# Queueing two more zero regions ahead of the first gradient store, in a decode backward kernel whose output is mostly zeros

## The chip, the cores and the metric

The kernel runs on one core of a Trainium2 chip. The metric is the device time of one execution in microseconds. A single core shows no second die to compare with, so "slow" here only means a run more than 1.5% above the fastest run of the same kernel in the same rounds. Profiles are of one execution each; the span in a profile is some 1.8 us shorter than the time of the same run.

## The reference, cut to what matters

The reference computes one decode step (attention over a cached window, then a gated feed-forward block) and all its gradients. Only the last 4096 of 32768 cache rows are attended to, so seven eighths of the two cache gradients are zeros, and they must be written.

```python
Hq, Hkv, Sk, Dh = 32, 8, 32768, 128            # B = 2
W = min(4096, max(256, Sk // 4))               # 4096
k = jnp.repeat(k_cache[:, :, Sk - W:, :], rep, axis=1)
v = jnp.repeat(v_cache[:, :, Sk - W:, :], rep, axis=1)
scores = jnp.einsum("bhqd,bhkd->bhqk", q, k) * (Dh ** -0.5)
...
_out, _vjp = jax.vjp(_f, A_x, A_k_cache, A_v_cache, A_wq, ...)   # out_2, out_3: cache gradients
```

Each cache gradient has 16 slabs (2 batches, 8 heads). A slab is 28672 rows of zeros, 7 MiB, and 4096 rows of numbers, 1 MiB. That makes 32 zero regions of 7 MiB, and 32 MiB of computed gradient.

## The kernel before

GpSimd issues the zeros as DMAs that read a small zero tile. The first 27 regions are issued early in the kernel. The other five are cut into 15 pieces that go out one behind each store of a computed gradient. Three regions (8, 16, 24) are cut into parts of different numbers of rows. The intent is to give some of the 16 DMA engines more 8 KiB packets than others; the traces have the size of each packet (8192 bytes) but not its engine, so which engine gets how many is not shown.

```python
OFF_DUP = OFF_WD                                   # scratch at 164 KiB
OFF_ST = [OFF_WG, OFF_WG + 16 * KIB] + [i * 16 * KIB for i in range(4)] + [OFF_WQ, OFF_WQ + 16 * KIB]
...                                                # second store buffer: 152 to 168 KiB
ZERO_PARTS = {8: (...), 16: (...), 24: ((4, 1), (15, 2), (2, 2), (15, 18), (12, 1), (P, 4), (16, 4))}
ZERO_FIRST, ZERO_CUTS = 27, (3, 2, 2)

def zero_cast(i):
    dst, done = zero_regions[i].bitcast(F32), 0
    for rows, n in ZERO_PARTS.get(i, ((P, ZPK // P),)):
        src = zt[0:rows * (P // rows):P // rows, :]
        nc.gpsimd.dma_start(out=dst[...].rearrange("(p k e) -> p k e", p=rows, k=n),
                            in_=src.unsqueeze(1).to_broadcast([rows, n, ZE]))
...
for i in range(ZERO_FIRST): zero_cast(i)           # at the start of attention(0)
...
for n, (b, what) in enumerate(jobs):               # 4 jobs: dV, dK of batch 0, then of batch 1
    ...
    for gq in range(2):
        ...                                        # 16 x 2 matmuls and evictions into two store buffers
        for a in range(2):
            nc.gpsimd.dma_start(out=dst_v[:, b, g0:g0 + 2, :, :], in_=sts[a][:])   # a store of 2 MiB
            zero_next()                                                            # a zero piece
        if gq == 0 and n + 1 < len(jobs):
            nxt = bd_of(n + 1)                     # block matrix of the next job, through OFF_DUP
```

## Time and profile before

| what | number |
|---|---|
| median of 6 runs | 802.67 us (791.57 to 809.69) |
| span of the profiled run | 797.8 us |
| DMA traffic, mean rate | 332.43 MB, 417 GB/s |
| first gradient store issued | 628.52 us |
| DMA engines idle or half idle around it | 604 to 632 us |

The page's part on DMA issues tells how far the zero stream runs ahead (operation, count, size of each, median time from issue to landing):

```profile
out_dram<-zt POOLq DMA_DIRECT2D x24, 7168.0 KB, 105.0
out_dram<-mem POOLq DMA_DIRECT2D x16, 2048.0 KB, 26.6
```

A 7 MiB region lands 105 us after its issue though the engines need only 17 us for it: it waits in the queue behind about five others. So the time at which a DMA is issued says little here about when its bytes move, and a queue that is empty (1 GB/s from 622 to 629.5 us) is worse than one that is long.

### The profile page before, as it was taken

The numbers are of one execution on the slowest core, as the hardware profiler recorded it, in microseconds if no ns is written. First come the engines' busy times: TensorE is split into PE (matmuls) and PEld (weight loads), VectorE is DVE, ScalarE is ACT, GpSimd is POOL, SyncE is SP. The second block draws the span as 40 slices with busy tenths as digits, with TensorE's granted clock in tenths as the row PEclk, the third lists the DMA queues.
The fourth block names the chain that finished last, engine by engine and source line by source line (L and its number), as shares of the span: only waits on it lengthen the run. The fifth ranks groups of instructions, "written<-read, shape, count | busy, mean of one in ns | idle before, by whom it ended". The sixth has DMA issues, their size and how long they took to land. (4 is left out here: it accounts for less than half of the span.)

```text
span 797.8 us, 12459 instructions
## 1 busy us (share of the span) xinstructions
PE 567.8 (71%) x5096; PEld 302.4 (38%) x5096; DVE 473.7 (59%) x1161; ACT 281.2 (35%) x406; POOL 65.7 (8%) x96
## 2 busy tenths in 40 slices
PE   3899997787688999832856879888796837811800
PEld 3656553455566555312425444433241212200200
DVE  1699998137433899740912577855447959922810
ACT  1534330135345343101102436553443826810800
POOL 4300000000020000000030000000000111210110
PEclk9999999777797999885976959865595968975955
DMA  8999999999999999999999999999999599999998
GB/s 365 419 418 421 420 425 427 422 430 427 427 420 420 424 424 423 426 425 431 427 427 429 428 426 428 425 426 426 430 428 403 222 429 427 428 429 430 427 430 347
DMA packets 41177, 332.43 MB, mean 417 GB/s; under 512 B 2192, under 2 KB 2208, under 8 KB 2336
## 3 DMA queue, kind: packets, MB, share of 16 engines
q0 software_dynamic: 34176, 268.44, 87.8%
q1 hardware_dynamic: 6932, 63.19, 34.9%
q8 instruction: 40, 0.66, 0.3%
q10 hardware_dynamic: 12, 0.01, 0.1%
q14 instruction: 17, 0.14, 0.0%
HBM read 49.30 MB, written 282.33 MB: 416 GB/s over the span
## 5 line engine op out<-in xcount | busy, mean ns | idle before, releaser
L422 DVE TENSOR_TENSOR mem<-mem,ee 128x512 bf16<-128x512 bf16 x512 | 180.7, 414 | 37.3 <-PE M_ps L433 36.9
L433 PE MATMUL M_ps<-mem 128*128 128x512 bf16 x512 | 139.6, 390 | 6.4 <-DVE mem L422 6.1
L93 ACT CAST mem<-ps_g 128x512 bf16<-128x512 f32 x128 | 74.3, 586 | 72.4 <-PE ps_g L836 65.7
L836 PE MATMUL ps_g<-mem 128*128 128x512 bf16 x256 | 82.5, 417 | 20.0 <-DVE mem L91 11.6
L380 ACT COPY mem<-KT_ps 128x1024 bf16<-128x1024 bf16 x64 | 63.4, 1013 | 80.9 <-PE KT_ps L378 75.1
L91 DVE CAST mem<-ps_g 128x512 bf16<-128x512 f32 x128 | 82.9, 687 | 6.8 <-ACT mem L93 4.0
L114 POOL DMA_DIRECT2D out_dram<-zt x45 | 35.5, 1029 | 503.7 <-DMA out_dram<-zt 503.4
L378 PE MATMUL KT_ps<-ident_bf,mem 128*128 128x128 bf16 x512 | 47.3, 238 | 30.9 <-DMA mem<-in_A_k_cache_dram 26.0
L254 PE MATMUL ps_tb<-ident_bf,mem 128*128 128x128 bf16 x480 | 56.2, 251 | 9.5 <-DMA mem<-in_B_w_gate_dram 2.8
L433 PEld LDWEIGHTS <-mem 128*128 128x128 bf16 x512 | 43.6, 99 | 49.0 <-issue 15.0
L836 PEld LDWEIGHTS <-mem 128*128 128x128 bf16 x256 | 25.9, 103 | 76.3 <-issue 56.7
L93 ACT COPY mem<-ps_tb 128x512 bf16<-128x512 bf16 x44 | 25.8, 586 | 70.8 <-PE ps_tb L254 66.0
L254 PEld LDWEIGHTS <-mem 128*128 128x128 bf16 x480 | 37.4, 128 | 34.9 <-issue 30.7
L378 PEld LDWEIGHTS <-mem 128*128 128x128 bf16 x512 | 35.5, 107 | 36.8 <-DMA mem<-in_A_k_cache_dram 26.6
L656 PE MATMUL VT_ps<-ident_bf,mem 128*128 128x128 bf16 x512 | 45.9, 237 | 2.4 <-ACT mem L93 1.1
L665 PE MATMUL dP_ps<-mem 128*128 128x512 bf16 x128 | 43.6, 429 | 4.7 <-ACT mem L93 4.7
L656 PEld LDWEIGHTS <-mem 128*128 128x128 bf16 x512 | 36.1, 106 | 27.0 <-issue 19.0
L93 ACT COPY mem<-VT_ps 128x1024 bf16<-128x1024 bf16 x31 | 31.7, 1022 | 34.8 <-PE VT_ps L656 33.6
L91 DVE COPY mem<-ps_tb 128x512 bf16<-128x512 bf16 x44 | 18.6, 424 | 41.9 <-PE ps_tb L254 40.5
L727 PE MATMUL ps_gr<-mem 2*128 2x512 bf16 (+1 forms) x78 | 33.4, 492 | 12.7 <-DVE mem L747 10.0
L91 DVE CAST mem<-ps_gr 128x512 bf16<-128x512 f32 (+1 forms) x38 | 24.8, 656 | 27.6 <-PE ps_gr L727 27.6
L91 DVE COPY mem<-VT_ps 128x1024 bf16<-128x1024 bf16 x33 | 23.1, 700 | 27.4 <-PE VT_ps L656 26.9
(244 smaller groups left out, 632.0 us busy)
## 6 DMA issues: line engine op xcount, KB each, us to landing
out_dram<-zt POOLq DMA_DIRECT2D x24, 7168.0 KB, 105.0
out_dram<-mem POOLq DMA_DIRECT2D x16, 2048.0 KB, 26.6
out_dram<-zt POOLq DMA_DIRECT2D x10, 2048.0 KB, 30.7
mem<-in_A_k_cache_dram SPq DMA_DIRECT2D x16, 1024.0 KB, 21.9
mem<-in_A_v_cache_dram SPq DMA_DIRECT2D x16, 1024.0 KB, 23.0
out_dram<-zt POOLq DMA_DIRECT2D x5, 3072.0 KB, 26.4
out_dram<-zt POOLq DMA_DIRECT2D x3, 4096.0 KB, 62.5
out_dram<-mem SPq DMA_DIRECT2D x5, 1792.0 KB, 18.8
```

The source lines that it names most:

```text
L91: nc.vector.tensor_copy(out=out, in_=in_)
L93: nc.scalar.copy(out=out, in_=in_)
L114: nc.gpsimd.dma_start(out=dst[done * ZE:(done + rows * n) * ZE].rearrange("(p k e) -> p k e", p=rows, k=n), in_=src.unsqueeze(1).to_broadc ...
L254: nc.tensor.transpose(out=ps[:, a, :], in_=src_block(a), identity=ident_bf[:])
L378: nc.tensor.transpose(out=KT_ps[:, jj, :], in_=Kt[b, g][:, u * 8 + jj, :], identity=ident_bf[:])
L380: nc.scalar.copy(out=KT[:], in_=KT_ps[:])
L422: nc.vector.tensor_tensor(out=pk[:, :, i, :].rearrange("p j (d t) -> p j d t", t=2), in0=Kb[:, j0:j0 + pk_j, :].rearrange("p j (d t) -> p ...
L433: nc.tensor.matmul(out=M_ps[:], lhsT=Vt[b, g][:, j, :], rhs=pk[:, jj, :, :].rearrange("p i d -> p (i d)"), start=(j == 0), stop=(j == NJ - 1))
L656: nc.tensor.transpose(out=VT_ps[:, jj, :], in_=Vt[b, g][:, a * 8 + jj, :], identity=ident_bf[:])
L665: nc.tensor.matmul(out=dP_ps[:, c, :], lhsT=dOpad[:, w0:w0 + P], rhs=VT[:, c * 4:(c + 1) * 4, :].rearrange("d a k -> d (a k)"), start=(i = ...
L727: nc.tensor.matmul(out=ps[:, :n], lhsT=lhsT_fn(k), rhs=rhs_fn(k), start=True, stop=True)
L836: nc.tensor.matmul(out=ps[:, a2, :], lhsT=lhs_bf[:, jp * P:(jp + 1) * P], rhs=rhs_bd[:, ap * 2 + a2, gq * 4:(gq + 1) * 4, :].rearrange("q ...
```

## The change

Its intent is to have bytes in the queue at the time when the compute has not yet produced the first gradient tile.

```diff
-    ... 24: ((4, 1), (15, 2), (2, 2), (15, 18), (12, 1), (P, 4), (16, 4))}
-    ZERO_FIRST, ZERO_CUTS = 27, (3, 2, 2)
+    ... 24: ((3, 16), (15, 2), (3, 4), (15, 18), (12, 2), (P, 4))}
+    ZERO_FIRST, ZERO_CUTS = 29, (1, 1, 1, 2, 2)
```

(The entries of regions 8 and 16 on the first line of each pair are unchanged and cut here.)

More of the change, by code (lines that the diff above doesn't have):

```diff
@@ L105 @@
     ZPK = Z * DH // 2 // ZE
-    ZERO_PARTS = {8: ((4, 1), (15, 2), (2, 2), (15, 14), (12, 2), (P, 4), (16, 7)), 16: ((4, 1), (15, 2), (2, 2), (15, 14), (12, 2), (P, 4), (16, 7)), 24: ((4, 1), (15, 2), (2, 2), (15, 18), (12, 1), (P, 4), (16, 4))}
-    ZERO_FIRST, ZERO_CUTS = 27, (3, 2, 2)
+    ZERO_PARTS = {8: ((4, 1), (15, 2), (2, 2), (15, 14), (12, 2), (P, 4), (16, 7)), 16: ((4, 1), (15, 2), (2, 2), (15, 14), (12, 2), (P, 4), (16, 7)), 24: ((3, 16), (15, 2), (3, 4), (15, 18), (12, 2), (P, 4))}
+    ZERO_FIRST, ZERO_CUTS = 29, (1, 1, 1, 2, 2)
     def zero_cast(i):
```

## The prediction

> **What bounds the kernel now.** I read the page's slices first, because the kernel writes two gradients that are mostly zeros: 332.43 MB of DMA traffic in a span of 797.8 us.
>
> ```profile
> DMA  8999999999999999999999999999999599999998
> GB/s 365 419 418 421 420 425 427 422 430 427 427 420 420 424 424 423 426 425 431 427 427 429 428 426 428 425 426 426 430 428 403 222 429 427 428 429 430 427 430 347
> q0 software_dynamic: 34176, 268.44, 87.8%
> ```
>
> The reader is to see a flat rate of about 427 GB/s in 36 of 40 slices. Only the first (loads begin), the last (the stream ends) and slices 31 and 32, at 598 to 638 us, fall below. At 427 GB/s the 332.43 MB need 778 us, so the DMA engines are the bound and the other engines' waits are mostly free. Only time in which the DMA engines stand still can be won. I therefore cut the stretch around the dip into windows (the last two columns are the DMA share and GB/s):
>
> ```profile
> 604.00:612.00 8.00, 5.97 (x14) 1.71 (x13) 5.65 (x8) 3.22 (x4) 0.00 (x0) 0.50 1.07 412
> 612.00:622.00 10.00, 7.48 (x18) 2.26 (x18) 8.59 (x11) 4.59 (x8) 0.00 (x0) 0.55 0.77 320
> 622.00:629.50 7.50, 6.59 (x23) 2.10 (x22) 7.18 (x12) 6.47 (x12) 0.98 (x2) 1.00 0.00 1
> 629.50:632.00 2.50, 2.28 (x9) 0.76 (x8) 2.29 (x5) 2.26 (x5) 1.90 (x3) 1.00 0.92 367
> 632.00:740.00 108.00, 51.80 (x160) 16.05 (x159) 65.73 (x97) 45.61 (x79) 14.16 (x20) 0.75 1.09 428
> 740.00:792.00 52.00, 16.19 (x56) 5.14 (x54) 18.48 (x30) 16.24 (x29) 4.99 (x7) 0.70 1.08 428
> 792.00:794.00 2.00, 0.00 (x0) 0.00 (x0) 0.00 (x0) 0.00 (x0) 0.00 (x0) 0.50 0.90 381
> ```
>
> The zeros run out between 612 and 622 us, unevenly over the engines; nothing moves for 7.5 us; then the rate is full again to 792. The gap, counted against 428: (16 x 8 + 108 x 10 + 427 x 7.5 + 61 x 2.5) / 428 = 4562 / 428 = 10.7 us. Who ends it stands in GpSimd's timeline (start, duration, operation, idle before and what ended it):
>
> ```profile
> 19.33 7.64 POOL L114 DMA_DIRECT2D out_dram<-zt  x8 [0.31 <-POOL zt L315]
> 556.44 1.84 POOL L114 DMA_DIRECT2D out_dram<-zt  x2 [21.94 <-DMA out_dram<-zt]
> 628.52 0.73 POOL L844 DMA_DIRECT2D out_dram<-mem  x1 [70.24 <-ACT mem L93]
> 664.06 0.71 POOL L844 DMA_DIRECT2D out_dram<-mem  x1 [22.11 <-ACT mem L93]
> 695.64 0.72 POOL L130 DMA_DIRECT2D out_dram<-zt  x1 [2.08 <-DMA out_dram<-zt]
> 748.82 0.71 POOL L844 DMA_DIRECT2D out_dram<-mem  x1 [30.39 <-ACT mem L93]
> ```
>
> The last two early zero regions are issued at 556.4 us. The first cache gradient store is issued at 628.5, when ScalarE has evicted its last tile. In between GpSimd has nothing to give. The first line also shows that eight issues go out at once and the later ones wait for landings: I take it that an issue waits for the eighth before it. Piece 9 at 695.64 fits: the eighth before it is piece 5, which ends 12 + 14 = 26 MiB after the first store begins, 629.7 + 26 x 2.45 = 693.4 us.
>
> Last, VectorE's timeline shows where the stores hold the compute back:
>
> ```profile
> 648.04 0.20 DVE L274 COPY mem<-qsT 128x128 bf16<-128x128 bf16 x1 [8.54 <-DMA out_dram<-mem]
> 732.21 0.20 DVE L274 COPY mem<-qsT 128x128 bf16<-128x128 bf16 x1 [29.52 <-DMA out_dram<-mem]
> ```
>
> The four jobs (dV, dK of each batch) need block matrices, built from a scratch at 164 KiB. That scratch lies inside the second of the eight store buffers (152 to 168 KiB), so it waits for store 1 to land (648.0), and for store 9 (732.2). Stores are numbered 0 to 15, four to a job.
>
> [...] In 606 to 610 us, where wq gradient stores of SyncE run beside the last zeros, the trace agrees that they share:
>
> ```profile
> q0 software_dynamic: 134, 1.09, 72.6%
> q1 hardware_dynamic: 81, 0.60, 35.7%
> ```
>
> [...]
>
> **The change part by part.** (1) Two regions of 7 MiB move ahead of the first store. A MiB takes 1.049 MB / 428 GB/s = 2.45 us, so they are 34.3 us of work. They cover the gap of 10.7 us and push all stores back by the rest. The bytes are the same. (2) Three regions remain; in pieces of 1, 1, 1, 2, 2 MiB they give 15 pieces, still one behind each of the first 15 stores, 21 MiB in place of 35. (3) Region 24 is cut anew. [...] A packet takes 8192 B / 26.75 GB/s = 0.31 us. [...] It is 46 early issues for 45.
>
> The intent of (3) follows from the windows: the gap today forgives imbalance. The engines that finish first, between 612 and 622, wait, and all start level at 629.7. Without the gap, an engine that is early stays early to the end, so it must be given more.
>
> Now the new order in time. Without a gap the work up to the first store would have ended at 629.7 - 10.5 = 619.2 us (10.5 is the gap without the last window's start). Two regions more: the stores' data start at S = 653.5. Then (2.46 us per MiB, which matches 67 MiB from 629.7 to 794.5 before, and 1.2 us from data to landing as at store 1):
> - store 1 has landed after 5 MiB: 653.5 + 12.3 + 1.2 = 667.0, not 648.0. VectorE's wait of 8.5 us becomes about 27; both jobs behind it move by 19 us.
> - store 4 followed that landing by 16.0 us (664.06 - 648.04), so it is issued at 683.0. The queue holds stores 0 to 3 and pieces 0 to 3, 13 MiB, until 685.5. Issue to first data is 1.2 us: margin 1.3 us.
> - store 9 has landed after 20 + 12 = 32 MiB: 733.4 or so, against 732.2. Its wait falls from 29.5 to about 12 us.
> - store 12 followed by 16.6 us: issued at 750.0. The queue holds 24 + 16 = 40 MiB, until 751.9. Margin 0.7 us after the first data.
> - the end: 53 MiB after S, 783.9, against 794.5 before.
>
> Eight in flight harms nothing: the last zeros can be issued from about 560 us, and store 3 needs region 27 landed (about 637), yet comes at 640. The sum on the path: -10.6 us; packets of region 24, 0 to -0.9; bubbles at stores 4 and 12, 0 to +2. On the profiled run that is about 788 of span.
>
> **The rivals.**
> (a) The slowest engine sets the end. Its gap is only from 622 to 629.7, 7.7 us, not the mean of 10.6. If region 24's packets go to the wrong engines, the win is 5 to 8 us, median about 796. For it: the tail, 381 GB/s in the last window, shows that one or two engines run longer than the rest. Against: it is only some 2 us after 165 us of equal shares, and the change reshuffles just these packets.
> (b) The stores become late, and the gap moves to store 4 or 12. For: margins of about 1 us. Against: both have their successors 1.3 us behind, so a bubble is 1 to 3 us and not 10. Median about 794.
> (c) The gap is larger than the profile's in the slow runs. The six times reach from 791.57 to 809.69 while the bytes are fixed. [...] The change allows the first store 24 us of delay at no cost, so slow runs would gain more, and the median would fall to 788 or less. Against: no view of the other runs.
>
> **Range and chances.** 802.67 - 10.6, with about 1 us back for (b) and 1.5 us off for (c), gives 791.5. Rival (a) and the scatter of 18 us in the times make the high side 800; (c) makes the low side 784. Two per cent is 16 us: more than the whole gap of 10.7, so only (c) gives "faster" by that much: 0.13. Nothing adds work, so slower is 0.01. Same: 0.86.
>
> **What would show it.** Right: no slice under 420 GB/s between 598 and 638 us; first store still issued near 628; VectorE waits of about 27 and 12 us at the two landings; the stream ends near 784; the page's mean near 422 GB/s. Wrong: a slice under 410 at 680 to 690 or 750 to 755 (b), or a last slice that tails off over 4 us or more at half rate (a). The prediction is wrong if the first store waits for a landing, which would be the eight in flight misread.

## The result, and the profile after

The changed kernel took 791.79 us (median of 10 runs, 791.60 to 792.35). The kernel before, now with 20 runs, took 800.34 (791.57 to 809.69). The ratio of the fast runs is 0.9922, with a 95% interval from 0.9891 to 0.9953. A ratio is the mean time of one kernel's fast runs over that of the other's in the same rounds, so it is not quite the ratio of the medians (0.9893): the runs of before over 803 us count as slow and are left out of it. It is faster, but by less than 2%. What the ratio hides is the scatter: 18 us before, 0.75 us after.

The slices of the page after:

```profile
DMA  8999999999999999999999999999999999999998
GB/s 364 418 419 421 418 426 426 423 429 428 429 419 420 424 425 422 427 424 431 427 429 427 427 428 428 430 422 424 427 429 430 422 428 429 387 428 426 430 395 356
```

The hole in slices 31 and 32 is gone (430 and 422 GB/s, where it was 403 and 222). Two small dips are new, in slices 35 and 39 (387 and 395). The same windows as before around the old gap, then those of the new dips and of the end (the last two columns are the DMA share and GB/s):

```profile
604.00:612.00 8.00, 5.80 (x13) 1.70 (x13) 5.65 (x8) 3.43 (x4) 0.00 (x0) 0.50 1.15 431
612.00:622.00 10.00, 7.46 (x19) 2.21 (x19) 8.76 (x12) 4.53 (x9) 0.00 (x0) 0.59 1.16 425
622.00:629.50 7.50, 6.69 (x23) 2.18 (x23) 7.27 (x12) 6.72 (x12) 1.43 (x3) 1.00 1.12 419
680.00:690.00 10.00, 7.12 (x25) 2.29 (x24) 9.75 (x15) 7.61 (x13) 2.70 (x4) 1.00 0.89 346
690.00:750.00 60.00, 36.34 (x113) 11.55 (x113) 43.84 (x65) 31.81 (x55) 7.89 (x12) 0.80 1.07 428
750.00:760.00 10.00, 8.65 (x31) 2.77 (x29) 9.59 (x16) 8.55 (x16) 2.68 (x4) 1.00 0.91 363
```

The new dips cost (82 x 10 + 65 x 10) / 428 = 3.4 us of the mean rate. GpSimd's timeline names what ends them:

```profile
557.14 2.90 POOL L114 DMA_DIRECT2D out_dram<-zt  x3 [21.50 <-DMA out_dram<-zt]
628.07 0.73 POOL L844 DMA_DIRECT2D out_dram<-mem  x1 [68.03 <-DVE mem L91]
657.76 0.68 POOL L130 DMA_DIRECT2D out_dram<-zt  x1 [15.88 <-DMA out_dram<-zt]
686.13 0.71 POOL L844 DMA_DIRECT2D out_dram<-mem  x1 [27.69 <-ACT mem L93]
753.96 0.72 POOL L844 DMA_DIRECT2D out_dram<-mem  x1 [27.60 <-ACT mem L93]
```

The last three early regions go out at 557 us. The first store comes at 628.07, within half a microsecond of before: the compute did not change, only what the queue holds. The issue at 657.76 is zero piece 3; the eighth issue before it is the last early region, and its landing releases it. Stores 4 and 12 (686.13, 753.96) are the ones that come too late and leave the dips. VectorE's two waits for the shared scratch are still there:

```profile
669.76 0.20 DVE L274 COPY mem<-qsT 128x128 bf16<-128x128 bf16 x1 [30.56 <-DMA out_dram<-mem]
737.00 0.20 DVE L274 COPY mem<-qsT 128x128 bf16<-128x128 bf16 x1 [12.75 <-DMA out_dram<-mem]
```

Comparing the two traces: 10.7 us of gap went, 3.4 us of new dips came, and 797.8 - 790.6 = 7.2 us of span were won. 10.7 - 3.4 = 7.3 fits, and I first took it for the explanation. The experiments show that it is a coincidence.

### The profile page after: what moved, and what is told of

It reads as the page before. It is cut to its first block, busy times and chain, and to the rows that moved or that the text cites.

```text
span 790.6 us, 12460 instructions
## 1 busy us (share of the span) xinstructions
PE 566.9 (72%) x5096; PEld 302.2 (38%) x5096; DVE 474.0 (60%) x1161; ACT 281.0 (36%) x406; POOL 65.7 (8%) x97
## 5 line engine op out<-in xcount | busy, mean ns | idle before, releaser
L836 PEld LDWEIGHTS <-mem 128*128 128x128 bf16 x256 | 25.9, 103 | 76.2 <-issue 56.7
## 6 DMA issues: line engine op xcount, KB each, us to landing
out_dram<-mem POOLq DMA_DIRECT2D x16, 2048.0 KB, 19.6
```

Source lines behind the costliest of these rows:

```text
L836: nc.tensor.matmul(out=ps[:, a2, :], lhsT=lhs_bf[:, jp * P:(jp + 1) * P], rhs=rhs_bd[:, ap * 2 + a2, gq * 4:(gq + 1) * 4, :].rearrange("q ...
```

## The experiments

All twelve kernels gave correct results (there is no e4). They ran on three chips; the median of the kernel before was 800.55, 799.58 and 800.15 us in them, so medians can be compared. Three theories are used. **S**: before the change, the time is that of the first store plus a constant. **M**: after it, the mean rate of the 16 DMA engines sets the end, so the dips cost 3.4 us. **L**: after it, the last single engine sets the end; it was still draining during the dips and lost nothing in them. Against S stands the rival that other engines' slack takes up a late store, and against L and M the rival that the new packet cut carries much of the gain.

| run | what it is | median us | first store us | span us |
|---|---|---|---|---|
| before | | 800.34 | 628.52 | 797.8 |
| after | | 791.79 | 628.07 | 790.6 |
| e1 | changed, old cut of region 24 | 792.18 | 627.82 | 790.3 |
| e2 | before, new cut of region 24 | 800.76 | 629.11 | 798.4 |
| e3 | changed, scratch moved | 791.85 | 635.48 | 790.1 |
| e5 | changed, pieces 1, 2, 2, 2 | 791.50 | 622.17 | 789.8 |
| e6 | 28 regions first, pieces 3, 2, 2 | 791.65 | 629.37 | 790.1 |
| e7 | before, first store late | 815.80 | 646.46 | 815.7 |
| e8 | changed, first store late | 791.66 | 645.69 | 790.6 |
| e9 | before, scratch moved | 793.74 | 622.76 | 792.1 |
| e10 | e5, meant to spare engine 4 8 packets more | 789.69 | 630.62 | 788.0 |
| e11 | changed, the same cut as e10 | 790.35 | 637.00 | 788.4 |
| e12 | e5, meant to give engine 4 8 packets more | 794.05 | 621.29 | 792.3 |
| e13 | e10, meant to give engines 0 to 2 12 more each | 793.41 | 622.77 | 791.5 |

First store and span are those of the profiled run of each.

### e1 and e2: the order alone, the cut alone

e1 is the changed kernel with this edit undone, and e2 is the kernel before with it:

```diff
-24: ((3, 16), (15, 2), (3, 4), (15, 18), (12, 2), (P, 4))
+24: ((4, 1), (15, 2), (2, 2), (15, 18), (12, 1), (P, 4), (16, 4))
```

> Undoes the new cut of region 24[...] and keeps the two regions ahead and the finer pieces. Theory (the covered gap is the whole gain, the cut only evens the engines): the gap at 612 to 630 us stays closed; [...]the median is 792.7, 0.9 us over the changed kernel's 791.79, and the tail of the stream is longer by that much. Rival 1 (the cut does nothing, the order is all): 791.8. Rival 2 (the cut carries much of the gain): 795 or more.

> Only the new cut of region 24, order and pieces of the kernel before. Theory: the gap forgives imbalance, the first store is still issued near 628 us whatever the engines did, so the median stays at 800 with the same scatter of some 18 us. Rival 2 (the cut carries much of the gain): 796 or less, at every run.

e1 took 792.18 us (792.06 to 792.33), e2 took 800.76 (800.09 to 801.46). So the order is the gain and the cut alone is nothing: rival 2 has fallen. The cut is worth 0.4 us at most in the changed order: the ten runs of the changed kernel reach from 791.60 to 792.35, so this is at the edge of the scatter. It is less than the 0.9 us expected, which is three packets of 0.31 us, and nearer to one packet; how many packets an engine has more or fewer by this cut was the author's estimate and is not shown. One thing I expected of e2 did not come: its four runs show no scatter of 18 us. Four runs are too few to tell luck from cause.

### e7 and e8: the first store late

```diff
+        if name == "bd0" and again:                          # again = 2
+            build_bd(off, rowsb, name, parts, again - 1)     # same values, written over again
         return dst
```

> The kernel before, but the first block matrix is built three times over (2 x 4 more VectorE multiplies of 1.16 us, 9.3 us), which delays the first store. Theory S (the DMA gap grows one for one with the first store's delay, and that is where the scatter comes from): first store near 638 us, gap near 20 us, median near 809, 9 us over the kernel before. Rival: other engines' slack takes it, median within 2 us of the kernel before.

> The changed kernel with the same delay of 9.3 us ahead of the first store. Theory S: the two regions ahead cover it (first store near 638 us, the zeros last to about 657), so the median stays at 791.8 within 0.5. Rival: the delay shows, 800.

The first store in the trace of e7, then in that of e8:

```profile
646.46 0.73 POOL L846 DMA_DIRECT2D out_dram<-mem  x1 [93.72 <-DVE mem L91]
```

```profile
645.69 0.73 POOL L846 DMA_DIRECT2D out_dram<-mem  x1 [86.89 <-DVE mem L91]
```

And the slices of e7:

```profile
GB/s 366 419 417 422 423 422 429 423 429 427 425 420 421 424 426 423 426 427 430 425 429 428 427 427 428 421 428 428 429 374 208 97 429 428 429 429 429 428 428 350
```

Both stores came some 18 us later than in the kernels they are made from. Some 8.5 us of that are the added multiplies; the rest was already there when the stage began that computes the gradient of wq, the last before the stores (its first eviction on VectorE was at 604.33 us in e7 and at 594.87 in the kernel before). This is the scatter of the earlier stages, which I had not put into the expected 809. The old order paid it in full: the span grew from 797.8 to 815.7, 17.9 us, for a store that is 17.9 us later, and the gap in the slices above grew with it (counted against 428 GB/s, 28.8 us; by the same count 10.8 before). The changed order paid nothing: 791.66. In all four profiles with the old order (before, e2, e7, e9) span minus first store is 169.2 to 169.3 us; in the changed order the first store moves from 622.17 to 645.69 and the span stays between 789.8 and 790.6 (e1, after, e3, e5, e6, e8). Theory S holds.

### e3, e5 and e6: three ways to close the new dips

```diff
-OFF_DUP = OFF_WD                                        # e3
+OFF_DUP = OFF_WD + 14 * KIB
-    ZERO_FIRST, ZERO_CUTS = 29, (1, 1, 1, 2, 2)         # e5
+    ZERO_FIRST, ZERO_CUTS = 29, (1, 2, 2, 2)
-    ZERO_FIRST, ZERO_CUTS = 29, (1, 1, 1, 2, 2)         # e6
+    ZERO_FIRST, ZERO_CUTS = 28, (3, 2, 2)
```

> The changed kernel with the 512-byte scratch of the block matrices moved from 164 KiB (inside the second store buffer) to 178 KiB, so VectorE no longer waits for stores 1 and 9 to land (30.6 and 12.8 us in the changed kernel's trace). All expect the waits gone and the slices at 680 to 690 and 750 to 760 us full (346 and 363 GB/s now). Theory M (the mean rate sets the end): those slices cost (82 x 10 + 65 x 10) / 428 = 3.4 us, so 788.4. Theory L (the last engine sets the end, and it did not idle in those bubbles because it was still draining): 791.0 to 791.8, with a longer tail instead.

> The changed kernel with the remaining three regions in pieces of 1, 2, 2, 2 MiB (12 pieces behind the first 12 stores) in place of 1, 1, 1, 2, 2. The queue then holds 2 MiB more when store 4 comes and 2 MiB more when store 12 comes, 4.9 us each, so both bubbles (1.9 and 1.5 us) should close without touching the waits. Theory M: 788.4. Theory L: 791.0 to 791.8. If 788.4 comes here but not with the moved scratch, or the other way round, neither theory holds alone.

> One region more ahead of the stores in place of two (28), the other four in pieces of 3, 2, 2 MiB; new cut of region 24 kept. 17.2 us of zeros cover the gap of 10.7 us with 6.5 us to spare, and the queue is 9 us deep when stores 4 and 12 come, so no bubble. Theory M (mean rate): 788.4. Theory L (last engine): 791.0 to 791.8. Theory S (the first store comes up to 8 us later in some runs): some runs at 793 or more.

All three closed both dips: after slice 7 no slice but the last is below 419 GB/s in any of them. These are e5's:

```profile
GB/s 365 417 417 422 421 425 427 422 429 428 428 421 419 423 425 424 426 424 430 427 428 428 428 428 429 421 428 425 427 428 428 421 432 429 425 427 428 429 421 309
```

All three took the time of the changed kernel: 791.85, 791.50 and 791.65. Theory M asked for 788.4 and has fallen. The end of e5 shows where the 3.4 us went (windows; one engine at full rate is 428 / 16 = 26.75 GB/s):

```profile
781.00:783.00 2.00, 0.00 (x0) 0.00 (x0) 0.00 (x0) 0.00 (x0) 0.00 (x0) 0.50 0.92 389
783.00:785.00 2.00, 0.00 (x0) 0.00 (x0) 0.00 (x0) 0.00 (x0) 0.00 (x0) 0.50 0.69 291
785.00:787.00 2.00, 0.00 (x0) 0.00 (x0) 0.00 (x0) 0.00 (x0) 0.00 (x0) 0.50 0.16 66
787.00:789.00 2.00, 0.00 (x0) 0.00 (x0) 0.00 (x0) 0.00 (x0) 0.00 (x0) 0.50 0.02 8
```

Engines drop out over 6 us, to some eleven at 783 to 785 and between two and three at 785 to 787. The same in the changed kernel:

```profile
784.00:786.00 2.00, 0.00 (x0) 0.00 (x0) 0.00 (x0) 0.00 (x0) 0.00 (x0) 0.50 0.99 422
786.00:788.00 2.00, 0.00 (x0) 0.00 (x0) 0.00 (x0) 0.00 (x0) 0.00 (x0) 0.50 0.67 283
788.00:790.00 2.00, 0.00 (x0) 0.00 (x0) 0.00 (x0) 0.00 (x0) 0.00 (x0) 0.50 0.02 8
```

There the full rate holds until 786 and ends almost at once. The last landing is at 788.95 us in this trace and at 788.12 in e5's, 0.8 us apart and not 3.4; the medians are 0.3 apart. So the dips had only made the quick engines wait for the slow one.

The trace holds this directly, though no view lists it: its semaphore records have 16 completions for each of GpSimd's DMAs, without the engine's name. For four transfers of 2 MiB in a row across the first dip of the changed kernel, the last of the 16 comes at 684.6, 689.6, 694.5 and 699.5 us, 5 us apart with no break. The first of the 16 comes at 676.3, 681.2, 692.9 and 697.8: the quickest engine stood still for some 7 us, the last one not at all.

Theory S's question in e6 stays open. Its four runs lie within half a microsecond, but only the first store of the profiled one is known (629.37 us). There are 6.5 us of zeros to spare, and perhaps none of the four had a store later than that.

### e9: the waits for the scratch, taken from the kernel before

> The kernel before with the scratch moved out of the store buffer (VectorE no longer waits 8.5 and 29.5 us for stores 1 and 9). The queue is full after 632 us in the kernel before, so nothing is to be won: median 800, the same scatter from 791 to 810. A rival that holds these waits to be on the path (the chain of waits gives 7% to them) expects 10 us or more less.

The edit is that of e3 on the kernel before. The four runs took 793.81, 793.67, 807.28 and 791.50 us; the third counts as slow. I expected 800. The first store of the profiled run:

```profile
622.76 0.73 POOL L844 DMA_DIRECT2D out_dram<-mem  x1 [64.17 <-ACT mem L93]
```

It came 5.8 us earlier, and 622.76 + 169.3 is the span of 792.1. So the time follows the store, not the waits that I took away. Nor, by the record, was it the moved scratch that made the store early. In e9 the scratch is first written at 387.3 us. By then the second attention stage had already waited 16.3 us for its last K load, in place of 25.5 in the kernel before; and e3, with the same move, waited 28.2 and had its first store at 635.48. The lines (what waits and for what: us in total, times, longest us) of e9, the kernel before and e3:

```profile
PE KT_ps L378 <- DMA mem<-in_A_k_cache_dram: 16.8, 2, 16.3
PE KT_ps L378 <- DMA mem<-in_A_k_cache_dram: 26.0, 2, 25.5
PE KT_ps L378 <- DMA mem<-in_A_k_cache_dram: 28.2, 1, 28.2
```

The profiled run was an early one, as e5's was at 622.17 without any moved scratch. The chain of waits, which gives 7% to "DMA out_dram<-mem", is no measure of what these waits are worth: e3 removed them in the changed order and won nothing.

### e10 to e13: which engine ends last

These cuts share the 896 packets of region 24 in other ways over the 16 engines. Against the changed kernel and e5, the cut of e10 and e11 is meant to spare the suspect, called engine 4 in the texts, eight packets more, and that of e12 to give it eight more. Against e10, the cut of e13 is meant to give three engines, called 0 to 2, twelve more each, and the others except engine 4 three fewer each (the eleven of the texts are those called 5 to 15). Which engine takes which packet was the author's estimate; no trace names the engine of a packet. What is measured is how far the end moves.

```diff
-24: ((3, 16), (15, 2), (3, 4), (15, 18), (12, 2), (P, 4))               # changed, e5
+24: ((3, 20), (15, 2), (3, 2), (15, 24), (12, 2), (P, 3), (16, 2))      # e10 (with 1, 2, 2, 2), e11
+24: ((3, 24), (15, 2), (3, 4), (15, 10), (12, 10), (P, 4))              # e12 (with 1, 2, 2, 2)
+24: ((3, 35), (15, 2), (3, 2), (15, 21), (12, 2), (P, 3), (16, 2))      # e13 (with 1, 2, 2, 2)
```

> Pieces of 1, 2, 2, 2 (no bubble; 791.50 with the new cut) [...] Theory L with engine 4 as the last engine: it ends 8 x 0.31 = 2.5 us earlier, the next engine (1.7 us ahead in that kernel's tail) takes over, so 789.8. If the last engine is another one: 791.5, no change. Theory M (mean rate): 791.5, no change, as the bytes are the same.

> Pieces of 1, 2, 2, 2, [...] Theory L with engine 4 last: 8 x 0.31 = 2.5 us later, 794.0, with one lone engine in the tail. Engine 4 not the last one: under 792.3.

> The same cut in the changed kernel itself (pieces 1, 1, 1, 2, 2, with its two bubbles). There 14 engines end 1.1 to 1.3 us before the last two (the last two 0.2 us apart), so sparing engine 4 alone can win 0.2 us[...], and 1.1 us if both late ones are spared: between 790.7 and 791.6. Less than e10 in any case, because here the bubbles hold the other engines back.

> As e10, [...] Five engines end 4 to 5 us early in the bubble-free tail; if engines 0 to 2 are among them, they take the 12 packets (3.7 us) and the eleven end 0.9 us earlier than in e10: 788.9. If they are not, they become the last: 791 or more.

(The tail figures in these texts are the 16 completions of the last DMA in the trace's semaphore records, read as one for each engine, without its name; e12 below fits that reading, with one of them open for 4.5 us and one engine's rate moved in that time.) The cut meant to take eight packets off gave 789.69 us, the one meant to add eight gave 794.05, where 789.8 and 794.0 were expected. The end of e12:

```profile
784.00:786.00 2.00, 0.00 (x0) 0.00 (x0) 0.00 (x0) 0.00 (x0) 0.00 (x0) 0.50 0.51 213
786.00:788.00 2.00, 0.00 (x0) 0.00 (x0) 0.00 (x0) 0.00 (x0) 0.00 (x0) 0.50 0.06 25
788.00:790.00 2.00, 0.00 (x0) 0.00 (x0) 0.00 (x0) 0.00 (x0) 0.00 (x0) 0.50 0.07 29
```

25 and 29 GB/s over 4 us is one engine working alone (26.75 at full rate). The last completion moved from 788.12 in e5 to 790.60, 2.48 us or 8 packets of 0.31 us, while the other 15 had come by 786.07. In the medians it is (794.05 - 791.50) / 8 = 0.32 us for each packet. The end of e10:

```profile
782.00:784.00 2.00, 0.00 (x0) 0.00 (x0) 0.00 (x0) 0.00 (x0) 0.00 (x0) 0.50 0.80 340
784.00:786.00 2.00, 0.00 (x0) 0.00 (x0) 0.00 (x0) 0.00 (x0) 0.00 (x0) 0.50 0.45 188
786.00:788.00 2.00, 0.00 (x0) 0.00 (x0) 0.00 (x0) 0.00 (x0) 0.00 (x0) 0.50 0.00 0
```

Here several engines end together and no lone one follows. Theory L holds: one engine ended last in e5, and the shifts fit that these cuts reached it, whatever its number is. e13 missed the hoped 788.9: it took 793.41, 3.72 us more than e10, and 12 x 0.31 is 3.7. This fits one of the three engines meant to have 12 packets more as the new last one; then it was not among the quick ones, and in e10 it was already at the end.

e11 took 790.35, 0.35 us below the range that I gave. I had left out that the last engine also sets when a store has landed, and so the dips. In e11 VectorE's wait for store 9 ended at 735.20 us in place of 737.00 and store 12 was issued at 751.46 in place of 753.96; the second dip is gone (429 GB/s in slice 39, where the changed kernel has 395) and the first is smaller (397 for 387). The quick engines then lost less in the dips, and all 16 ended at 785.12 to 786.70 us, for 787.58 to 788.95 in the changed kernel. That sparing the last engine brought the landings forward is the likeliest reading, but the cut of e11 moves other packets too, and no run separates them.

e10 beats both kernels: 789.69 us, 2.1 us less than the changed kernel, and a fast-run ratio to the kernel before of 0.9885 (0.9849 to 0.9920; recorded as "unclear" at the 2% mark).

## Why the prediction was right or wrong, point by point

**The number and the class were right**, 791.5 for 791.79 and "same". Part of the closeness is luck, as the terms show.

**The bound, and what ends the gap: right.** e7 shows it to a tenth of a microsecond: the old span is the first store plus 169.3 us.

**"The sum on the path: -10.6 us" failed.** It takes the mean rate of 16 engines for the end of the stream, 783.9 us; the full rate held until 786 and the span shrank by 7.2, not 10.6. The term is mis-sized: rival (a) had the right quantity, the 7.7 us for which the last engine stood idle between 622 and 629.7 (the last landing of the stream moved from 796.20 to 788.95, 7.25 us). That rival was written as a risk of a bad cut; it was the rule. Its "median about 796" was too high, because it starts from a six-run median that held three late runs, and their larger gap went as well (c). The sign that it named, a tail of 4 us or more, did not come: the dips kept the other engines level with the last one, and only the runs without dips (e3, e5, e6) show the tail.

**The landings came late for the same reason.** Predicted and found: store 1 landed at 667.0 and 669.8, store 9 at 733.4 and 737.0, stores 4 and 12 issued at 683.0 and 686.1, at 750.0 and 754.0. Each is 3 to 4 us late. A landing came with the last of its 16 completions, while the queue's end was worked out from the mean. The 16 completions of store 1 show it: they come from 661.6 to 669.7 us (VectorE's wait for this store ended at 669.76), with a mean of 666.7, where 667.0 was predicted; in the kernel before, where all engines had started level at 629.7, they lay within half a microsecond (647.5 to 648.0). The spacing behind a landing was right (16.4 us to store 4, for 16.0).

**Rival (b), bubbles of 0 to 2 us with about 1 us on the end: half right.** They came, at both places, 3.4 us together. They cost 0 to 0.3 us in the medians, because the engine that sets the end never idled in them (e3, e5, e6, and the completions across the first dip).

**Region 24, "0 to -0.9": right**, 0.4 us, near the scatter. The 0.9 stood for three packets of 0.31 us fewer on eleven engines, the author's estimate; one packet (0.31 us) would fit better, but no trace shows which engine has how many, and no run separates the two.

**Rival (c), the slow runs gain more: right, and larger than its weight of 1.5 us.** The changed kernel does not have the scatter. e7 and e8 show the mechanism: 18 us of lateness cost 17.9 and 0. That each slow run of the kernel before had a late store is not seen, as only their times are known, but the record fits it well. The 52 runs of that kernel fall into three groups: 5 at 791.6 to 793.5 us, 31 at 798.6 to 801.8, 16 at 805.6 to 811.3. The first stores of the twelve profiles without an added delay do so too: 621.3 to 622.8, 627.8 to 630.6, 635.5 to 637.0. With 169.3 us after the store and 1.8 from span to time, these stores would give 792.4 to 793.9, 798.9 to 801.7 and 806.6 to 808.1. The granted clock does not tell the groups apart: where it is on record, it is 0.798 in the one run of the first group and 0.804 and 0.799 in the mean of the other two.

**Luck.** The starting point was off: the 6 runs had a median of 802.67, 20 runs 800.34. So 802.67 less 11.2 arrived at the result through a gain 2.6 us too large (the medians moved by 8.55) and a start 2.3 us too high.

**Eight in flight: right.** The first store did not wait, and piece 3 was released at 657.76 by the landing of the last early region.

**Still open:** why the first store comes in three groups, some 7 us apart. The traces place it: the second attention stage waits for its last K load 16.3 to 19.6 us in the four profiles with an early store (e5, e9, e12, e13), 24.4 to 25.9 in the six of the middle group, 28.2 and 28.3 in the two late ones (e3, e11). From the first eviction of the wq gradient stage to the first store it is 33.4 to 33.8 us in all twelve. What makes that load slow or quick was not tested.

## What to carry to other kernels

When the DMA engines are the bound, look for the moments when their queue runs dry, and put work that depends on nothing in front of the work that depends on compute; here this also took the run-to-run scatter of the compute off the time (18 us before, 0.75 us after). Once the queue never ran dry in this kernel, the mean rate of 428 GB/s no longer predicted the end (783.9 us by it, the last landing at 788.95): the engine that ended last did, and closing the dips in the mean rate won nothing (791.85, 791.50 and 791.65 us for 791.79), as that engine was busy in them. It also set when a store had landed (store 1 at 669.8 us, where 667.0 was predicted), and so when what waits for the landing could go on. Then look for the engine that ends last, and test it by giving it a few packets more and a few less: the cut meant to add eight moved the last landing by 2.48 us here.
